# Moving half of the first MLP weight to the head of the load stream of a decode kernel

## The chip, the core and the metric

The kernel runs on one core of a Trainium2 chip. The metric is device time in microseconds (us). The kernel before takes 77.36 us, the median of 13 runs that lie between 77.12 and 78.14 us. The execution that the profiler recorded took 77.22 us; the recorded span, from the first instruction to the last, is 75.5 us.

The engines are called as the profile calls them: PE is the matrix engine (PEld its weight loads), DVE the vector engine, ACT the scalar engine, POOL the general one, and SP the engine that here does nothing but issue DMAs. Sixteen DMA engines of the core move what the DMA instructions ask for; "SPq" is SP's queue of issuing instructions.

## The reference

One decode step for a batch of four tokens with 512 features. The input is layer-normed; the result goes through two branches, and the output is `x + s * g`:

- attention `s`: `q = xn @ wq` gives 32 query heads of 128; 8 key/value heads serve four query heads each. Only the last 1024 of 4096 cached positions are used. Scores `q·k / sqrt(128)`, softmax, product with V, and `@ wo`, a 4096 x 512 matrix.
- MLP gate `g`: the input is normed once more, `h = gelu(y @ w1 + b1)` with `w1` 512 x 1792, `silu(h @ w2 + b2)` with `w2` 1792 x 512.

All arrays are bf16. What has to be read from DRAM is about 28.8 MB: 8 K blocks and 8 V blocks of 1 MB each, `wq` and `wo` of 4 MB each, `w1` and `w2` of 1.75 MB each, and some vectors.

## The kernel before

The program is a list of operations for each engine, in the order in which the Python code adds them; `add` puts one on a compute engine, `dma` one on the queue of an issuing engine, each with the operations it depends on. There is no scheduler: an engine runs its list from top to bottom, and `emit` puts a wait ahead of an operation for every dependency on another engine or a DMA.

All large loads are issued by SP, so their order is the order of the load stream. Before the change it is K0, K1 (L216, L217), the two halves of `wq` (L219), K2 to K7 (L221), V0 (L440), `w1` whole (L441), V1 (L443), `w2` (L444), V2 to V7 (L446), and `wo` in six pieces (L453), the last of them small. K and V share eight buffers of 1 MB: V of head g is loaded into the buffer that held K of head g, so its issue waits for the last transposes of that K block (L214). Nothing else in the stream before the output waits for a compute engine. ACT issues the small loads.

A K block has 128 partitions, each holding 32 consecutive positions of one batch entry, a contiguous 8 KB row in DRAM. The four partitions next to each other are the four batch entries, 8 MB apart in DRAM. `w1` is laid out with four rows of the matrix to a partition: 14 KB contiguous in DRAM, one partition behind the other.

PE's list is:

1. eight transpose units T(0) to T(7) (K0 and K1, four units of eight 128x128 transposes each, L279), copied to SBUF by DVE (L285);
2. the transposes of the normed input (L347);
3. the query product in two halves, each waiting for its half of `wq` (L362), copies of the result by DVE and ACT (L368, L369), and its transposes (L374);
4. 32 pairs of T(n) and S(n-8): a unit of transposes, and the score matmuls of a unit that was transposed eight units earlier (L294 sets the mask, L298 multiplies); the exponential of a head's scores is taken by ACT (L306);
5. for each head g, PV(g) (L316) and the sum of the probabilities (L322), with DVE's epilogue one head behind (L329 to L334). Behind PV(0) stands the first MLP product (L392, L394), which waits for `w1`; behind PV(1) the second one (L419, L421), which waits for `w2`;
6. a rearrangement of the attention result (L465, copied at L472), and the product with `wo`, one group of matmuls for each of its six pieces (L486), each waiting for its piece;
7. the gate, a transpose, the residual and the output DMA (L512 to L520).

The two lines of the wait that ties the V loads to PE, and those of the `w1` load and its only reader:

```python
            kv_buf[:, (HKV + g) % NS, :, :].rearrange("p c d -> p (c d)"), cache_rows(A_v_cache, g)),
            t_last[(HKV + g) % NS] if HKV + g >= NS else None)
...
    d_w1 = pg.dma("sp", "w1", lambda e: e.dma_start(
        w1_sb[:, :, :], B_w1.rearrange("(p c) f -> p c f", c=4)))
...
        t = add("pe", fn, v_xyT, d_w1, d_b1)
```

Of the kernel before, what the change touches and what calls it, by code (L numbers as in the profile page):

```python
# [16 lines left out]
class _Program:  # L17
# [10 lines left out]
    def add(self, eng, fn, *deps):  # L28
        op = _Op(eng, fn, deps)
        self.ops[eng].append(op)  # L30
        return op
# [42 lines left out]
def bass_recurrent_scan__sliding_block_cached__mixer_channel_mlp__decode_kernel(  # L74
# [48 lines left out]
    w1_sb = sb([128, 4, F], BF16)  # L123
# [63 lines left out]
    pg = _Program(nc)  # L187
    add = pg.add
# [3 lines left out]
    d_b1 = pg.dma("act", "b1", lambda e: e.dma_start(  # L192
        b1_sb[0:1, :], B_b1.rearrange("(o n) -> o n", o=1)))
# [3 lines left out]
    def cache_rows(cache, g):  # L197

        return bass.AP(cache.tensor, g * SK * DH + WS * DH,
                       [[NC * DH, KR], [HKV * SK * DH, B], [1, NC * DH]])  # L200
# [5 lines left out]
    def load_k(g):  # L206
        d_k[g] = pg.dma("sp", "k%d" % g, lambda e: e.dma_start(  # L207
            kv_buf[:, g, :, :].rearrange("p c d -> p (c d)"), cache_rows(A_k_cache, g)),
            )

    def load_v(g):
        d_v[g] = pg.dma("sp", "v%d" % g, lambda e: e.dma_start(  # L212
            kv_buf[:, (HKV + g) % NS, :, :].rearrange("p c d -> p (c d)"), cache_rows(A_v_cache, g)),
            t_last[(HKV + g) % NS] if HKV + g >= NS else None)  # L214

    load_k(0)  # L216
    load_k(1)  # L217
    wq_r = A_wq.rearrange("(p c) n -> p c n", c=4)
# [120 lines left out]
    v_xyT = None  # L339
# [14 lines left out]
    v_xyT = add("dve", lambda e: e.tensor_copy(yT[:, :], psK[1][:, 16:32]), t_xy)  # L354
# [31 lines left out]
    def mlp1():  # L386
        def fn(pe):
            last = None
            for k in range(FC):
                o = psM[:, PS_H + k * 4:PS_H + (k + 1) * 4]  # L390
                for c in range(4):
                    pe.matmul(o, bass.AP(w1_sb, c * F + k, [[4 * F, 128], [FC, 128]]),  # L392
                              yT[:, c * 4:(c + 1) * 4], start=(c == 0), stop=False)
                last = pe.matmul(o, bass.AP(b1_sb, k, [[F, 1], [FC, 128]]), ones_bf[0:1, 0:4],  # L394
                                 start=False, stop=True)
            return last
        h = psM[:, PS_H:PS_H + FC * 4]
        t = add("pe", fn, v_xyT, d_w1, d_b1)
        a = add("act", lambda e: e.activation(u2_sb[:, :], h, AF.Square), t)  # L399
        v = add("dve", lambda e: e.tensor_scalar(t_sb[:, :], u2_sb[:, :], GELU_K, 1.0,  # L400
                                                 op0=ALU.mult, op1=ALU.add), a)
        v = add("dve", lambda e: e.tensor_tensor(t2_sb[:, :], t_sb[:, :], h, ALU.mult), v)
        mlp["e"] = add("act", lambda e: e.activation(ge_sb[:, :], t2_sb[:, :], AF.Exp,
                                                     scale=-GELU_A), v)
# [31 lines left out]
    for n in range(LAG, NUN + LAG):  # L436
# [1 line left out]
            T(n)  # L438
        S(n - LAG)
    load_v(0)  # L440
    d_w1 = pg.dma("sp", "w1", lambda e: e.dma_start(  # L441
        w1_sb[:, :, :], B_w1.rearrange("(p c) f -> p c f", c=4)))
    load_v(1)  # L443
    d_w2 = pg.dma("sp", "w2", lambda e: e.dma_start(  # L444
        w2_sb[:, :, :], B_w2.rearrange("(p c) o -> p c o", c=FC)))
# [49 lines left out]
    for g in range(HKV):  # L495
        PV(g)
        if g == 0:
            mlp1()
        if g >= 1:
            epilogue(g - 1)  # L500
        if g == 1:
            mlp2()
            mlp3()
        if g == 2:
            mlp4()
    epilogue(HKV - 1)
    rows = to_rows(0, HKV)
    for k in range(len(d_wo)):
# [7 lines left out]
    t = add("pe", lambda pe: pe.transpose(psS[0][0:16, 0:128], sg_sb[:, :], ident32[:, :]),  # L516
            v, c_id32, ex[HKV - 2])
# [56 lines left out]
```

## Time and profile before

| | us |
|---|---|
| median of 13 runs | 77.36 |
| lowest and highest run | 77.12, 78.14 |
| the profiled execution | 77.22 |
| its span | 75.5 |
| PE busy | 55.2 |
| DVE busy | 38.1 |
| ACT busy | 9.0 |

The DMA engines' packets of SP's queue fill 91.7% of the span of sixteen engines, and 28.85 MB are read from DRAM, 382 GB/s over the span. The page divides the span into 40 slices; each digit is the busy share of an engine in a slice, in tenths. The row PEclk is the clock that PE was granted, in tenths of full speed. A waiting instruction is shown with the idle time ahead of it and, behind an arrow, with what ended it; "issue" stands for time in which the profile shows nothing that the engine waits for.

### The profile page before, as it was taken

The page shows a single profiled execution, that of the slowest core. Times are in us where ns is not written, and L with a number is a line of the kernel's source. Part 1 is how long each engine was busy: PE and PEld are TensorE (multiplying, and loading weights), DVE is VectorE, ACT ScalarE, POOL GpSimd, SP SyncE. Part 2 cuts the span into 40 slices and gives each one's busy share as a digit, 9 for nine tenths or more (in the row PEclk, how much of TensorE's full clock was granted, in tenths as well). Part 3 has the DMA queues.
Part 4 walks back from the last instruction along what each step waited for, and adds up shares of the span by engine and source line. Part 5 has one row for each costly group of instructions (what it writes and reads, how often), then busy time and mean ns, then how long its engine had stood idle before and what let it go on. Part 6 is the DMA issues. An engine that isn't in the chain of part 4 may idle for free.

```text
span 75.5 us, 2408 instructions
## 1 busy us (share of the span) xinstructions
PE 55.2 (73%) x1107; PEld 47.0 (62%) x1107; DVE 38.1 (50%) x84; ACT 9.0 (12%) x16; POOL 4.5 (6%) x13
## 2 busy tenths in 40 slices
PE   0009994603689999999999909999299999728850
PEld 0009993201078999999998809999098675428730
DVE  0678988100323999999985000003943968850010
ACT  0611000000360213203204400002000000000000
POOL 6970000000000000000000000000000000000000
PEclk9999999996555999999999985555555555555555
DMA  0899999999999999999999999999999999999600
GB/s 2 275 404 417 445 452 425 425 425 395 430 425 430 425 417 438 417 430 449 428 394 451 422 433 396 425 417 425 430 425 434 408 408 425 410 415 422 249 15 2
DMA packets 4213, 28.99 MB, mean 384 GB/s; under 512 B 486, under 2 KB 619, under 8 KB 1644
## 3 DMA queue, kind: packets, MB, share of 16 engines
q1 hardware_dynamic: 4160, 28.84, 91.7%
q8 instruction: 8, 0.13, 0.6%
q10 hardware_dynamic: 44, 0.01, 0.1%
q14 instruction: 1, 0.01, 0.0%
HBM read 28.85 MB, written 0.00 MB: 382 GB/s over the span
## 4 chain that ended last, share of the span: by engine, by line
DMA 49%; PE 25%; SPq 21%; issue 1%; DVE 1%
DMA kv_buf<-in_A_k_cache_dram 25%; DMA wo_sb<-in_A_wo_dram 24%; SPq L454 17%; PE psK L279 16%; PE psS L298 6%; PE psS L294 2%; SPq L207 2%; SPq L219 1%; PE psM L486 1%; PE psS L516 1%; SPq L212 0%; DVE o_bf L518 0%; DVE sg_sb L512 0%
## 5 line engine op out<-in xcount | busy, mean ns | idle before, releaser
L279 PE MATMUL psK<-ident,kv_buf 128*128 128x128 bf16 x256 | 21.6, 241 | 5.9 <-DMA kv_buf<-in_A_k_cache_dram 5.8
L285 DVE COPY kt_buf<-psK 128x1024 bf16<-128x1024 bf16 x32 | 21.0, 688 | 2.8 <-PE psK L279 2.7
L279 PEld LDWEIGHTS psK<-ident,kv_buf 128*128 128x128 bf16 x256 | 17.5, 109 | 6.3 <-DMA kv_buf<-in_A_k_cache_dram 6.1
L298 PE MATMUL psS<-qT,kt_buf 128*128 128x16 bf16 x256 | 10.3, 170 | 0.0
L298 PEld LDWEIGHTS psS<-qT,kt_buf 128*128 128x128 bf16 x256 | 9.5, 97 | 1.1 <-issue 0.3
L316 PEld LDWEIGHTS psO<-P_buf,kv_buf 128*128 128x128 bf16 x256 | 7.7, 103 | 2.2 <-issue 1.9
L316 PE MATMUL psO<-P_buf,kv_buf 128*128 128x16 bf16 x256 | 8.2, 174 | 0.3
L392 PE MATMUL psM<-yT,w_sb 128*128 128x4 bf16 x56 | 5.7, 204 | 1.8 <-issue 1.8
L306 ACT ACTIVATE P_buf<-psS 128x512 bf16<-128x512 f32 x8 | 4.8, 597 | 16.1 <-PE psS L298 16.1
L329 DVE TENSOR_REDUCE den_sb<-psS 128x16 f32<-128x512 f32 x8 | 5.5, 688 | 1.7 <-PE psS L322 1.4
L392 PEld LDWEIGHTS psM<-yT,w_sb 128*128 128x128 bf16 x56 | 4.5, 153 | 2.3 <-issue 2.1
L400 DVE TENSOR_SCALAR t_sb<-u_sb 128x56 f32<-128x56 f32 x1 | 0.2, 192 | 11.4 <-ACT u_sb L399 11.4
L362 PE MATMUL psO<-wq_sb,xT 128*32 128x512 bf16 x32 | 2.9, 505 | 3.8 <-DMA wq_sb<-in_A_wq_dram 3.5
L486 PE MATMUL psM<-OW,wo_sb 128*128 128x4 bf16 x128 | 4.0, 166 | 1.5 <-DMA wo_sb<-in_A_wo_dram 1.0
L486 PEld LDWEIGHTS psM<-OW,wo_sb 128*128 128x128 bf16 x128 | 3.7, 104 | 1.8 <-DMA wo_sb<-in_A_wo_dram 1.2
L322 PE MATMUL psS<-P_buf,ones_bf 128*128 128x512 bf16 x8 | 4.5, 561 | 0.0
L362 PEld LDWEIGHTS psO<-wq_sb,xT 128*32 128x32 bf16 x32 | 0.8, 112 | 5.1 <-DMA wq_sb<-in_A_wq_dram 4.0
L368 DVE CAST q_sb<-psO 128x512 bf16<-128x512 f32 x1 | 0.7, 690 | 6.5 <-PE psO L362 6.5
L294 PE MATMUL psS<-negm,ind 128*128 128x512 bf16 x8 | 3.3, 410 | 0.0
L419 PE MATMUL psM<-hT,w_sb 128*128 128x4 bf16 x56 | 2.1, 167 | 1.4 <-DVE hT L411 1.4
L394 PE MATMUL psM<-ones_bf,b_sb 1*128 1x4 bf16 x14 | 3.0, 215 | 0.0
L419 PEld LDWEIGHTS psM<-hT,w_sb 128*128 128x128 bf16 x56 | 1.8, 105 | 1.9 <-DVE hT L411 1.9
(63 smaller groups left out, 28.7 us busy)
## 6 DMA issues: line engine op xcount, KB each, us to landing
kv_buf<-in_A_k_cache_dram SPq DMA_DIRECT2D x8, 1024.0 KB, 21.4
kv_buf<-in_A_v_cache_dram SPq DMA_DIRECT2D x8, 1024.0 KB, 23.7
wq_sb<-in_A_wq_dram SPq DMA_DIRECT2D x2, 2048.0 KB, 13.3
w_sb<-in_B_w_dram SPq DMA_DIRECT2D x2, 1792.0 KB, 31.0
wo_sb<-in_A_wo_dram SPq DMA_DIRECT2D x3, 1024.0 KB, 24.9
wo_sb<-in_A_wo_dram SPq DMA_DIRECT2D x1, 512.0 KB, 21.5
wo_sb<-in_A_wo_dram SPq DMA_DIRECT2D x1, 384.0 KB, 18.2
wo_sb<-in_A_wo_dram SPq DMA_DIRECT2D x1, 128.0 KB, 18.0
```

The lines of the kernel that those rows point to most:

```text
L279: last = pe.transpose(psK[n % NB][:, j * 128:(j + 1) * 128], kv_buf[:, g, u * UT + j, :], ident[:, :])
L285: cp[n] = add("dve", lambda e: e.tensor_copy(kt_buf[:, n % NKT, :], psK[n % NB][:, 0:1024]), t, sc.get(n - NKT))
L294: pe.matmul(psS[g % 2][:, 0:512], ind[:, :], negm[:, :], start=True, stop=False, skip_group_check=True)
L298: last = pe.matmul(psS[g % 2][:, c * 16:(c + 1) * 16], kt_buf[:, n % NKT, j * 128:(j + 1) * 128], qT[:, g * 16:(g + 1) * 16], start=False, ...
L306: ex[g] = add("act", lambda e: e.activation(P_buf[:, g, :], psS[g % 2][:, 0:512], AF.Exp, scale=SCALE), sc[n])
L316: last = pe.matmul(pso[:, 0:16], kv_buf[:, (HKV + g) % NS, c, :], P_buf[:, g, c * 16:(c + 1) * 16], start=(c == 0), stop=(c == NC - 1))
L322: den[g] = add("pe", lambda pe: pe.matmul(psS[g % 2][:, 0:512], ones_bf[:, :], P_buf[:, g, :], start=True, stop=True), ex[HKV - 2 + g % 2] ...
L329: v = add("dve", lambda e: e.tensor_reduce(den_sb[:, cs], bass.AP(psS[g % 2], 0, [[512, 128], [1, 16], [16, NC]]), AX.X, ALU.add), den[g])
L392: pe.matmul(o, bass.AP(w1_sb, c * F + k, [[4 * F, 128], [FC, 128]]), yT[:, c * 4:(c + 1) * 4], start=(c == 0), stop=False)
L419: pe.matmul(o, w2_sb[:, k, c * 128:(c + 1) * 128], hT[:, k * 4:(k + 1) * 4], start=(k == 0), stop=False)
L454: e.dma_start(wo_sb[:, g0:g1, i0:i1, :], wo_r[:, g0:g1, i0:i1, :]))))
L486: last = pe.matmul(psM[:, PS_W + c * 4:PS_W + (c + 1) * 4], wo_sb[:, g, i, c * 128:(c + 1) * 128], OW[:, i, g * 4:(g + 1) * 4], start=firs ...
```

## The change

The load of `w1` is cut in two DMAs of two matrix rows to a partition (7 KB in DRAM and in SBUF for each of the 128 partitions). The first is issued by SP ahead of everything else, before K0. The second stays at the place of the old load, between V0 and V1. The first MLP product now waits for both. No compute instruction changes or moves in its engine's list.

```diff
+    w1_r = B_w1.rearrange("(p c) f -> p c f", c=4)
+
+    def load_w1(c):
+        return pg.dma("sp", "w1%d" % c, lambda e: e.dma_start(
+            w1_sb[:, 2 * c:2 * c + 2, :], w1_r[:, 2 * c:2 * c + 2, :]))
+
+    d_w1 = [load_w1(0)]
     load_k(0)
     load_k(1)
...
-        t = add("pe", fn, v_xyT, d_w1, d_b1)
+        t = add("pe", fn, v_xyT, *d_w1, d_b1)
...
     load_v(0)
-    d_w1 = pg.dma("sp", "w1", lambda e: e.dma_start(
-        w1_sb[:, :, :], B_w1.rearrange("(p c) f -> p c f", c=4)))
+    d_w1.append(load_w1(1))
     load_v(1)
```

## The prediction

> **What bounds the kernel now.** I read the page's busy slices and DMA part first, then the stretches, the chain of waits, the list of PE's waits, and the timeline at the places they point to.
>
> ```profile
> span 75.5 us, 2408 instructions
> ...
> PE   0009994603689999999999909999299999728850
> ...
> DMA  0899999999999999999999999999999999999600
> ...
> q1 hardware_dynamic: 4160, 28.84, 91.7%
> ```
>
> The DMA row is full from the second slice to the 36th: the load stream hardly pauses, and its end is close to the kernel's end. Bytes do not change, so a gain can come only from the rate. The stretches (us, busy times by engine, granted clock, DMA share, GB/s) show where the rate is low:
>
> ```profile
> 2.00:8.00 6.00, 2.25 (x22) 2.25 (x23) 4.79 (x13) 1.69 (x3) 3.12 (x6) 1.00 1.03 394
> 8.00:17.00 9.00, 5.30 (x69) 4.31 (x67) 4.89 (x10) 0.00 (x0) 0.00 (x0) 1.00 1.00 426
> 26.00:40.00 14.00, 13.95 (x323) 13.24 (x321) 12.97 (x20) 2.98 (x5) 0.00 (x0) 1.00 1.01 424
> 53.00:70.00 17.00, 13.08 (x340) 10.23 (x340) 10.20 (x31) 0.18 (x1) 0.00 (x0) 0.50 1.01 419
> ```
>
> Only the opening is slow: 394 against 426 GB/s over 6 us is 6 x (1 - 394/426) = 0.45 us of stream. K and V blocks run at 424 later on, `wo` (4 KB rows and shorter, with some V) at 419.
>
> The chain that ended last, in order of time (start, us, what), and PE's own list of waits:
>
> ```profile
> 3.30 18.67 DMA kv_buf<-in_A_k_cache_dram
> ...
> 22.02 1.03 PE psK L279 x8
> 23.06 0.43 PE psS L294
> 23.48 0.20 PE psS L298 x8
> ...
> 24.70 0.46 PE psK L279 x8
> ...
> 53.90 18.20 DMA wo_sb<-in_A_wo_dram
> ```
>
> ```profile
> PE psK L279 <- DMA kv_buf<-in_A_k_cache_dram: 5.8, 1, 5.8
> PE psO L362 <- DMA wq_sb<-in_A_wq_dram: 3.5, 1, 3.5
> ...
> PE psM L486 <- DMA wo_sb<-in_A_wo_dram: 1.0, 3, 0.4
> ```
>
> PE waits for data three times: for K0 at the start, for the second half of `wq` (until 18.19 us), and for `wo` at the end. Between 18.19 and the first `wo` group it waits for no V block, no `w1`, no `w2`: one long chain of matmuls and DVE copies. So there are two chains, the stream and the matmuls, and the last wait tells how far apart they end. The timeline of the end:
>
> ```profile
> 67.71 1.84 PE L486 MATMUL psM<-OW,wo_sb 128*128 128x4 bf16 x64 [0.51 <-DVE OW L472]
> 69.97 1.01 PE L486 MATMUL psM<-OW,wo_sb 128*128 128x4 bf16 x32 [0.42 <-DMA wo_sb<-in_A_wo_dram]
> 71.20 0.59 PE L486 MATMUL psM<-OW,wo_sb 128*128 128x4 bf16 x16 [0.21 <-DMA wo_sb<-in_A_wo_dram]
> 72.15 0.59 PE L486 MATMUL psM<-OW,wo_sb 128*128 128x4 bf16 x16 [0.36 <-DMA wo_sb<-in_A_wo_dram]
> ```
>
> The stream wins, but only by 0.42 + 0.21 + 0.36 = 0.99 us. If the matmul chain comes later by more than 0.99 us, it sets the end.
>
> **The change, part by part.**
>
> *The 7 KB rows ahead of K0.* Half of `w1` is 917,504 bytes; at 426 GB/s that is 2.15 us. K0, K1, both halves of `wq` and K2 to K7 land 2.15 us later; from V1 on the stream stands where it stood. This delays what the matmul chain starts on: the second half of `wq` released PE at 18.19 us, and K2 landed at 3.30 + 18.67 = 21.97, just before T(8) at 22.02. Both move, so neither absorbs the shift. +2.15 us on the matmul chain.
>
> *What `w1` buys.* Nothing waits for it before. Its load was issued at 9.96 us and took 31.0 us to land, at 40.9; the first product's first matmul ran at 43.13. The 1.83 us gap of PE at 45.12, put down to "issue", lies behind that first matmul, which had already read `w1`, so it is no wait for the load. Gain 0.
>
> *One more DMA on SP.* An issue of this size takes 0.6 us (two K issues in 1.25 us), ahead of K0 and of each later issue. The 2.15 us of transfer of the new first load cover it; without that cover K0 would be 0.6 us later. V0's issue waits for T(3) and moves from 9.38 to about 11.5 us; it took 27 us from issue to landing, so what hides it is a backlog of more than 20 us. The same holds at the end: V7's issue at 40.06 waits for PE's last transposes and goes to about 42.2, and the `wo` issues behind it move too; they landed 18.0 us or more after issue, which leaves 16 us. ACT's and POOL's queues have nothing moved.
>
> *Shorter rows.* The two halves are 256 rows of 7 KB in place of 128 of 14 KB. Between the rows at 426 GB/s and those at 419, 1.8 MB cost 0 to 0.07 us; I take 0.03.
>
> *The opening.* The loss of 0.45 us may belong to K0's and K1's rows, as the first loads: then `w1` in front cures it, -0.45. It may belong to whatever opens the stream: 0. Or `w1`'s opening loses as much and K's does too: +0.45. The nearest row, K blocks of the same layout at 424 GB/s in 26 to 40 us, says that the layout loses nothing by itself, so I take 0.
>
> [...]
>
> *The matmul clock.* The stretches at one microsecond give the granted clock's switches (the clock is the third number from the end of a line):
>
> ```profile
> 17.00:18.00 1.00, 0.00 (x0) 0.00 (x0) 0.00 (x0) 0.00 (x0) 0.00 (x0) 0.76 0.88 369
> 24.00:25.00 1.00, 1.00 (x23) 1.00 (x20) 0.45 (x1) 0.00 (x0) 0.00 (x0) 0.83 1.03 434
> 44.00:45.00 1.00, 0.00 (x0) 0.00 (x0) 0.00 (x0) 0.00 (x0) 0.00 (x0) 0.91 0.97 416
> ```
>
> With two levels, 1.0 and 0.5, the clock fell at 17.52, rose at 24.34 and fell at 44.82; the distances 6.82 and 20.48 are 1 to 3, so the switches may lie on a grid of 6.8 us or a fraction of it. From 18.19 to 24.34 the chain runs 6.15 us at half clock. There a pair of T and S costs 1.03 + 0.20 = 1.23 us against 0.46 + 0.18 = 0.64 later: each microsecond at half clock loses 0.48. If the switches move along with the work: 0. If they stay on a grid of half of 6.82, the slow stretch may last from 3.4 to 6.8 us: -1.3 to +0.3, on average -0.5. I take half of that, -0.25.
>
> [...]
>
> *Sum.* Matmul chain: +2.15 + 0.03 - 0.25 = +1.93; less the 0.99 us that it was early: +0.94 us at the end. The stream itself: 0 to 0.05. The profiled execution's 77.22 becomes 78.16; it lies 0.14 below the median of 77.36, against which I put the forecast at 78.2.
>
> **The rivals.** A difference within 0.5% (0.39 us) is about what a measurement of this kernel cannot tell from no change.
>
> *Faster: the clock comes back one step sooner.* Place: 18 to 26 us. Price: 3.41 x 0.48 = -1.6 us on the matmul chain, more than the +1.19 by which it would otherwise be late (2.15 + 0.03 - 0.99). Then the stream sets the end again, and a cured opening shows: 77.36 - 0.45 = 76.9. It decides from 1.19/0.48 = 2.5 us less at half clock. For it: 6.15 us is near the top of what the grid allows. Against it: it needs the opening cured as well, for which only 0.45 us are there.
>
> *Hidden anyway.* The same, with the opening as slow as before, or a late chain of less than 0.4 us: 77.0 to 77.7, say 77.4.
>
> *Not what it says.* `w1` in front opens as badly and the clock stays low one step more: 2.18 - 0.99 + 1.6 = +2.8, 80.1. [...]
>
> **How the numbers follow.** Matmul chain late and deciding: 0.60, with 77.75 to 78.8 (the upper end: 77.36 + 1.19 + 0.3 for the clock). Hidden anyway: 0.22. Faster: 0.15. Slow twice: 0.03. The range that holds 8 in 10 goes from 76.95, the case of a cured opening, to 78.85; the likeliest case's own is 77.75 to 78.8. Faster by over 0.5%: 0.15; within: 0.23; slower: 0.62.
>
> **What the profile after would show.** PE's wait for the second half of `wq` ends near 20.3 us instead of 18.19, the wait for K0 near 7.9 instead of 5.75. The first `wo` group starts between 69 and 70.2 us instead of 67.71, and PE no longer waits 1.0 us for `wo`, or hardly. The last piece of `wo` still lands between 71.8 and 72.6 us. The stretch from 2 to 8 us tells of the opening: 394 GB/s again if it belongs to any first load, some 415 or more if K0 at the head was the cause. The prediction is wrong if the `wo` waits are still there: then either the chain started less late than 2.15 us, or the half-clock stretch was shorter by 2.5 us.

## The result, and the profile after

The changed kernel is slower: the ratio to the kernel before is 1.0114, with a 95% interval of 1.0067 to 1.0162, so 77.36 us become about 78.2 us. A second measurement on another occasion gave 1.0102 (1.0035 to 1.0169). The ratios leave out the runs classed as slow, and these are most runs of the changed kernel: over all 11 timed ones its median is 79.15 us (77.73 to 80.36), against 77.36 us (77.05 to 78.93) in 48 runs of the kernel before. So the loss is 0.9 us by the ratio and 1.8 us by all runs, and the changed kernel spreads over 2.6 us, where the kernel before spreads over 1.9.

The profiled execution of the changed kernel is its best: 77.28 us, a span of 75.6 us, hardly more than the 77.22 and 75.5 us of the kernel before. Its time does not show the loss, but its lines show what decides now. From the page:

```profile
span 75.6 us, 2409 instructions
...
PE   0000799470278999999999982999929999946970
...
DMA  1899999999999999999999999999999999999500
...
q1 hardware_dynamic: 4304, 28.84, 91.8%
...
PE 60%; DMA 23%; DVE 7%; issue 4%; SPq 3%; ACT 0%
DMA wq_sb<-in_A_wq_dram 23%; PE psK L286 16%; PE psO L323 8%; PE psS L305 8%; PE psM L399 6%; PE psM L492 5%; PE psS L329 4%; PE psM L401 3%; PE psS L301 3%; PE psM L426 3%; PE psO L369 3%; DVE den_sb L336 2%; SPq L207 2%; PE psK L381 1%; DVE q_sb L375 1%
```

The stream is as full as before (91.8% against 91.7%). But the chain that ended last runs over PE for 60% of the span, and its only transfer is `wq`; before, the last piece of that chain was `wo` and 24% of the span. PE's waits (what waited, for whom, us in total, times, longest) and the timeline of the query product and of `wo`:

```profile
PE psK L286 <- DMA kv_buf<-in_A_k_cache_dram: 8.1, 1, 8.1
PE psO L369 <- DMA wq_sb<-in_A_wq_dram: 3.4, 1, 3.4
```

```profile
20.29 1.90 PE L369 MATMUL psO<-wq_sb,xT 128*32 128x512 bf16 x16 [3.38 <-DMA wq_sb<-in_A_wq_dram]
...
69.06 3.69 PE L492 MATMUL psM<-OW,wo_sb 128*128 128x4 bf16 x128 [0.51 <-DVE OW L478]
```

The wait for `wo` is gone. All 128 matmuls of `wo` run in one piece of 3.69 us, and their data has landed before they are due. K0 releases PE 2.31 us later than before (8.06 against 5.75), the second half of `wq` 2.10 us later (20.29 against 18.19), T(8) 1.80 us later (23.82 against 22.02), and the first `wo` group starts 1.35 us later (69.06 against 67.71). The stretches:

```profile
2.00:8.00 6.00, 0.00 (x0) 0.00 (x0) 4.55 (x12) 1.63 (x3) 3.12 (x6) 1.00 0.94 377
8.00:17.00 9.00, 7.50 (x88) 6.53 (x88) 5.58 (x10) 0.00 (x0) 0.00 (x0) 1.00 1.03 440
26.00:40.00 14.00, 14.00 (x324) 13.41 (x322) 12.89 (x20) 2.98 (x5) 0.00 (x0) 0.98 1.01 423
53.00:70.00 17.00, 13.60 (x343) 10.44 (x343) 11.02 (x33) 0.65 (x3) 0.00 (x0) 0.50 1.01 418
```

The rates are those of before, within what a stretch's borders do. (The 377 GB/s from 2 to 8 us are neither of the two values that the prediction named; the stream starts before 2 us now, and its borders no longer fit this stretch.) From 0 to 17 us the mean is 371 GB/s against 365, which is 0.1 MB or 0.24 us ahead; the last piece of `wo` landed 14.7 us after its issue at 57.53, at 72.2, against 54.38 + 18.0 = 72.4 before. The stream gained 0.2 us that nobody waits for.

### The profile page after: what moved, and what is told of

It reads as the page before. It is cut to its first block, busy times and chain, and to the rows that moved or that the text cites. A ratio compares the mean times of both kernels' runs of the same rounds, so it can differ in the third digit from the quotient of the medians.

```text
span 75.6 us, 2409 instructions
## 1 busy us (share of the span) xinstructions
PE 54.4 (72%) x1107; PEld 46.7 (62%) x1107; DVE 38.5 (51%) x84; ACT 9.0 (12%) x16; POOL 4.5 (6%) x13
## 3 DMA queue, kind: packets, MB, share of 16 engines
q1 hardware_dynamic: 4304, 28.84, 91.8%
## 4 chain that ended last, share of the span: by engine, by line
PE 60%; DMA 23%; DVE 7%; issue 4%; SPq 3%; ACT 0%
DMA wq_sb<-in_A_wq_dram 23%; PE psK L286 16%; PE psO L323 8%; PE psS L305 8%; PE psM L399 6%; PE psM L492 5%; PE psS L329 4%; PE psM L401 3%; PE psS L301 3%; PE psM L426 3%; PE psO L369 3%; DVE den_sb L336 2%; SPq L207 2%; PE psK L381 1%; DVE q_sb L375 1%
## 6 DMA issues: line engine op xcount, KB each, us to landing
wo_sb<-in_A_wo_dram SPq DMA_DIRECT2D x3, 1024.0 KB, 24.1
```

## The experiments

Two theories besides the late matmul chain (theory 1) had to be told apart: that the extra DMA and its shorter rows slow the stream (theory 2), and that any load but K0 at the head opens it badly (theory 3).

**The two halves, but both at the old place.**

```diff
-    d_w1 = [load_w1(0)]
+    d_w1 = []
...
+    d_w1.append(load_w1(0))
     d_w1.append(load_w1(1))
```

> The first MLP weight is cut in the same two DMAs of 7 KB rows, but both stand where the whole load stood, between V0 and V1. Theory 1 (the data that the matmul chain starts on come 2.15 us later, and the chain sets the end): nothing is ahead of K0, so no difference from before, 77.2 to 77.5 us, PE waits about 1.0 us for wo. Theory 2 (the extra DMA and its shorter rows slow the stream): as slow as the changed kernel, 78 to 79 us, with the last piece of wo landing later than 72.4 us. Theory 3 (the stream opens differently): no difference here.

77.38 us, ratio 1.0013 (0.9993 to 1.0032): the cut by itself costs nothing that shows, and theory 2 falls. But the profile isn't what was expected. PE did not wait for `wo` there; the second half of `wq` released it at 19.72 us instead of 18.19, though nothing in the stream ahead of it differs from before. The two `wq` loads' time from issue to landing, before and here:

```profile
DMA to landing us min/median/max: 11.1/13.3/15.4
```

```profile
DMA to landing us min/median/max: 11.1/14.0/16.9
```

The first half landed equally fast, the second 1.5 us later. A load lands in 16 shares, each with its own time in the trace; 15 of this one had landed by 18.09 us, the last one at 19.68. A 16 KB packet of the instruction queue (the page counts it to the same sixteen DMA engines) starts in this execution at 17.6 to 17.7 us, before the second half is in; in the kernel before it starts at 18.0 to 18.1, when the second half is nearly in, and there K2's last share is the late one (21.98 against 20.59 us for the fifteenth). That the packet makes the share late fits in time: in all thirteen profiles no load ahead of the first such packet has a last share more than 0.5 us behind the fifteenth, and the load that is landing at the packet, or the next one, has one 0.8 to 1.6 us behind. But the packet itself took only 0.96 us here, and moving it wasn't tried, so the cause is not shown.

The half-clock stretch is longer as well. The clock is the third number from the end:

```profile
17.00:18.00 1.00, 0.00 (x0) 0.00 (x0) 0.00 (x0) 0.00 (x0) 0.00 (x0) 0.94 0.97 401
28.00:29.00 1.00, 0.95 (x24) 0.88 (x22) 0.99 (x2) 0.60 (x1) 0.00 (x0) 0.94 1.04 442
```

By the two-level reading it fell at 17.9 and rose at 28.1: 10.2 us, against 6.8 before. So this execution's chain was late by 1.5 us and some slow microseconds more, and ended the kernel instead of the stream: a span of 75.9 us against 75.5, with the load order of before.

**How much of the weight goes first.** A quarter (the cut after one matrix row of four), and the whole weight as one DMA:

```diff
-    def load_w1(c):
+    def load_w1(c, cut=1):
+        lo, hi = ((0, cut), (cut, 4))[c]
...
-            w1_sb[:, 2 * c:2 * c + 2, :], w1_r[:, 2 * c:2 * c + 2, :]))
+            w1_sb[:, lo:hi, :], w1_r[:, lo:hi, :]))
```

```diff
-            w1_sb[:, 2 * c:2 * c + 2, :], w1_r[:, 2 * c:2 * c + 2, :]))
+            w1_sb[:, :, :], w1_r[:, :, :]))
...
-    d_w1.append(load_w1(1))
```

> Only one of the four matrix rows of a partition (3.5 KB rows, a quarter of the weight) opens the stream, the other three follow between V0 and V1. Theory 1: the second half of wq lands 1.08 us later than before instead of 2.15; the chain was 1.0 to 1.3 us early, so the end is 77.2 to 77.8 us, with PE's waits for wo down to 0.3 us or less. Theory 3 (any foreign first load costs, by how the stream opens): the same loss as with half of the weight, 78 to 79 us.

> The whole weight opens the stream (14 KB rows, one DMA, the number of DMAs as before). Theory 1: the second half of wq lands 4.3 us later than before, near 22.5 us; chain late by 4.3 - 1.3 = 3.0 us, so 80.0 to 81.5 us, with no wait for wo left. Theory 2 (an extra DMA, shorter rows): no more DMAs and no shorter rows than before, so 77.4 us. Theory 3: as the changed kernel, 78 to 79 us.

The quarter: 78.06 us, ratio 1.0101 (1.0051 to 1.0151). The whole: 82.03 us, ratio 1.0608 (1.0549 to 1.0666). The whole has no more DMAs than before and its old rows, which settles theory 2, and it costs far more than half does, against theory 3, by which the loss should not depend on the amount. The quarter's time alone would fit theory 3, as it loses what the half loses; its profile and the two next experiments speak for theory 1. But the quarter lost more than theory 1 gave it, and so did the whole (4.7 us against an expected 2.6 to 4.1). The profiles show the same two additions as above. PE's query product and `wo` in the two kernels, quarter first:

```profile
20.66 1.90 PE L370 MATMUL psO<-wq_sb,xT 128*32 128x512 bf16 x16 [5.20 <-DMA wq_sb<-in_A_wq_dram]
...
69.53 3.69 PE L493 MATMUL psM<-OW,wo_sb 128*128 128x4 bf16 x128 [0.51 <-DVE OW L479]
```

```profile
24.68 1.90 PE L369 MATMUL psO<-wq_sb,xT 128*32 128x512 bf16 x16 [5.30 <-DMA wq_sb<-in_A_wq_dram]
...
74.17 3.55 PE L491 MATMUL psM<-OW,wo_sb 128*128 128x4 bf16 x128 [0.51 <-DVE OW L477]
```

20.66 is 18.19 + 1.08 + 1.4, and 24.68 is 18.19 + 4.3 + 2.2. The half-clock stretch behind it ends at 27.9 and at 31.7 us, 7.2 and 7.0 us after `wq`'s release instead of 6.15. In both the last share of the second half of `wq` landed well behind the other fifteen (20.62 against 19.15 us, and 24.64 against 23.05), with an instruction packet that starts at 18.1 and at 22.6 us.

**A late chain with the stream of before.** Ten matmuls that nobody reads, reckoned as 2.1 us at half clock (2.3 us in the profile), ahead of the rearrangement:

```diff
+    def f_late(pe):
+        last = None
+        for _ in range(10):
+            last = pe.matmul(psM[:, 256:512], ones_bf[:, :], negm[:, 0:256], start=True, stop=True)
+        return last
+    add("pe", f_late, ep[HKV - 1])
     rows = to_rows(0, HKV)
```

> The kernel before, its load stream untouched, with ten matmuls of 256 columns (read by nobody) on PE behind the last head's epilogue, ahead of the rearrangement and wo: at half clock 10 x 0.21 = 2.1 us on the matmul chain, as much as the change puts on its start. Theory 1 (a late matmul chain is enough): slower by 2.1 less the 1.0 to 1.3 us that the chain was early, 78.2 to 79.2 us, no wait for wo left. Rival (the loss is in the stream, not in PE): 77.4 us.

78.73 us, ratio 1.0166 (1.0095 to 1.0237): as expected. In the profile `wo` starts 2.7 us later than before (70.42), more than the ten matmuls took, because the second half of `wq` was 1.3 us late here too (19.50). PE waits for no piece of `wo`, and the last piece landed at 72.2, no later than before. A late chain is enough for a loss of this size, with the load stream left as it was.

**The late data with a shorter chain.** In both kernels half of the first MLP product's matmuls are left out, so the output lacks half of that sum:

```diff
-                for c in range(4):
+                for c in range(2):
                     pe.matmul(o, bass.AP(w1_sb, c * F + k, [[4 * F, 128], [FC, 128]]),
```

> The kernel before with the first MLP product over two of the four matrix rows of a partition (28 of its 56 matmuls left out, so the output lacks half of that sum; the load stays whole). It takes some 2.5 us off the matmul chain and nothing off the stream. Theory 1: the stream sets the end as before, 77.2 us, with the slowest runs gone; PE waits for wo for 2 to 3 us.

> The changed kernel with the same 28 matmuls left out (the output lacks half of that sum; both loads stay). Theory 1: the chain is 2.15 us late and 2.5 us shorter, the stream sets the end again, so 76.9 to 77.4 us: within 0.4 us of the kernel before with the same cut, and some 1.5 us under the changed kernel. Rival (the stream itself has become slower): 78 us or more, with wo's last piece landing late. What is left between this and the other cut kernel is what the new opening is worth to the stream alone.

With the order of before 77.14 us (77.05 to 77.26), ratio 0.9960 (0.9933 to 0.9987); with the changed order 77.41 us (77.09 to 78.85), ratio 0.9998 (0.9956 to 1.0041). So the changed load order costs 0.3 us by the medians once the chain is shorter, instead of 0.9 to 1.8 us, and most of the loss isn't in the stream. PE waits for `wo` again, in the changed order with the cut by less than in the order of before:

```profile
PE psM L492 <- DMA wo_sb<-in_A_wo_dram: 0.6, 2, 0.4
```

```profile
PE psM L486 <- DMA wo_sb<-in_A_wo_dram: 1.1, 3, 0.5
```

The 2 to 3 us of waiting that I expected of the cut kernel of before are 1.1, in part because this execution's clock rose only at 25.9, 1.55 us later than in the kernel before, or some 0.7 us of work. Two more things follow. The kernel before, too, is held up by its matmul chain in some runs: with the chain cut it loses 0.4% and its upper tail. And the gain of 0.2 us in the opening doesn't show here: in the two profiles the last piece of `wo` landed at 72.4 us with the order of before and at 72.7 with the changed one.

**Matmuls in the gap.** The changed kernel, with 24 matmuls of 256 columns on constants between the halves of the query product:

```diff
+    def f_warm(pe):
+        last = None
+        for _ in range(24):
+            last = pe.matmul(psM[:, 256:512], ones_bf[:, :], negm[:, 0:256], start=True, stop=True)
+        return last
+    add("pe", f_warm, c_neg)
     t_q = add("pe", lambda pe: f_q(pe, 1), d_wq[1])
```

> The changed kernel with 24 matmuls of 256 columns on constants (their result is read by nobody) between the two halves of the query product, where PE waits for the second half of wq; they take 2.6 us at full clock, inside the gap of 3.4 us. Theory 1 with the clock: the half-clock stretch of some 6 us behind the gap goes, the chain gains up to 6.2 x 0.48 = 2.9 us, more than it is late; PE waits for wo again and the time is 77.0 to 77.4 us, with little spread. If the clock isn't what spreads the runs: 78 to 79 us as without them. If the matmuls themselves delay the chain: above 79 us.

78.52 us, ratio 1.0182 (1.0116 to 1.0248): a miss. The gap was filled and the second half of the product took 1.05 us instead of 1.90, but the timeline goes on like this:

```profile
20.35 1.05 PE L369 MATMUL psO<-wq_sb,xT 128*32 128x512 bf16 x16 [0.36 <-DMA wq_sb<-in_A_wq_dram]
22.20 0.62 PE L388 MATMUL psK<-ident,q_sb 128*128 128x128 bf16 x8 [0.80 <-DVE q_sb L382]
23.77 0.76 PE L286 MATMUL psK<-ident,kv_buf 128*128 128x128 bf16 x8 [0.96 <-DMA kv_buf<-in_A_k_cache_dram]
24.75 0.40 PE L305 MATMUL psS<-qT,kt_buf 128*128 128x16 bf16 x8 [0.22 <-issue]
25.01 1.01 PE L286 MATMUL psK<-ident,kv_buf 128*128 128x128 bf16 x8
```

What was gained was lost at once in a wait for K2, T(8) starting at 23.77 as in the changed kernel (23.82), and the clock fell afterwards, at 24.1, for 3.4 us. Behind that this execution lost more: `wo` starts at 69.96 against 69.06, and PE's gaps put down to "issue" are 2.4 us at PV, where the changed kernel has 1.7 us at the first MLP product. So the run neither frees the chain of the clock nor tells what a freed chain would do.

**Work in the gap instead.** What PE needs late should come late, and what it waits for early. K0 and K1 are not used until the query exists; so the first half of `wq` opens the stream, then come K0, K1, and the second half, and PE transposes K0 and K1 in the gap. The essence (T(1) and the query's transposes get the waits that their shared buffer then needs):

```diff
+    d_wq = [load_wq(0)]
     load_k(0)
     load_k(1)
+    d_wq.append(load_wq(1))
...
-    for n in range(LAG):
-        T(n)
...
     add("pe", lambda pe: f_q(pe, 0), v_xT, d_wq[0])
+    for n in range(LAG):
+        T(n)
     t_q = add("pe", lambda pe: f_q(pe, 1), d_wq[1])
```

> The kernel before with the first half of wq as the first load, then K0, K1, the second half of wq and the rest as it was; on PE the small transposes and the first half of the query product stand ahead of T(0), which is behind them. Nothing that the chain needs lands later than before at 18.2 us, K0 and K1 land 4.9 us later, and PE transposes them in the gap in which it waited for wq, so that gap is filled. Theory 1 with the clock: the half-clock stretch behind 18.2 us shrinks or goes, the chain is earlier by 1 to 3 us, the stream decides: 77.0 to 77.3 us, few slow runs. If any load of another kind than K at the head costs (theory 3): 78 us or more.

> The kernel in which the first half of wq opens the stream, once more, for its interval: 0.3 to 0.7% faster than before, 77.0 to 77.3 us, PE waits for wo by 1 us or more, full clock at 18 us.

77.15 us, ratio 0.9948 (0.9914 to 0.9982), and again 77.25 us, ratio 0.9978 (0.9953 to 1.0003): 0.2 to 0.5% under the kernel before (the second interval just reaches no change), with nothing above 77.8 us. The first profile, in which the clock stayed at 1.0 from 14.6 to 45.3 us, shows what it buys:

```profile
8.53 1.90 PE L364 MATMUL psO<-wq_sb,xT 128*32 128x512 bf16 x16 [0.45 <-DMA wq_sb<-in_A_wq_dram]
18.10 1.05 PE L364 MATMUL psO<-wq_sb,xT 128*32 128x512 bf16 x16 [1.74 <-DMA wq_sb<-in_A_wq_dram]
67.04 1.84 PE L490 MATMUL psM<-OW,wo_sb 128*128 128x4 bf16 x64 [0.51 <-DVE OW L476]
```

The chain is 0.67 us earlier at `wo` (67.04 against 67.71) and PE waits 1.4 us for it. So the stream bounds the kernel here, and an earlier chain can gain no more. In the second profile the clock did fall, for 6.8 us, and the wait was 1.0 us. A foreign load at the head that does not make the chain late costs nothing, which is against theory 3 once more.

**The 2.15 us once more, in that order.** Half of `w1` ahead of it, the other half at the old place (shown against the kernel just above):

```diff
+    d_w1 = [load_w1(0)]
     d_wq = [load_wq(0)]
     load_k(0)
```

> Half of the first MLP weight opens the stream as in the changed kernel, then the first half of wq, K0, K1, the second half of wq and the rest; PE's order as in the run in which wq opens. The data of the chain come 2.15 us later as in the changed kernel, but the gap ahead of the query product is filled with the transposes of K0 and K1, so it should run at full clock. Theory 1 with the clock: the chain, 1.4 to 1.8 us early in that run, becomes 0.3 to 0.8 us late: 77.3 to 78.0 us, under the changed kernel by 1 us or so. If only the 2.15 us count and not the clock: as the changed kernel, 78.3 to 79.2 us.

> The changed kernel once more, beside the next two on the same chip. Theory 1: 78 to 79.5 us, PE waits for no piece of wo, the second half of wq releases PE at 20.3 us or, where an instruction fetch of 16 KB sits in the queue of one DMA engine ahead of it, up to 1.5 us later; the half-clock stretch behind it lasts 6.8 or 10.2 us. The time follows these two: with 6.8 us and 20.3 near 77.3, with both bad near 80.

Side by side on one chip: 77.93 us with the filled gap, ratio 1.0024 (0.9974 to 1.0075), against 78.86 us of the changed kernel, ratio 1.0102 (1.0035 to 1.0169). The `wq` half came as late in both (20.76 and 20.35 us), and what differs is that K0 and K1 come behind the first half of `wq` and fill PE's gap, and the clock with it: in the profile of this kernel it is 1.0 from 16.9 to 47.6 us. Each run's mean granted clock is on record: the five of its ten runs with 0.808 or more took 77.21 to 77.78 us, the five with 0.780 or less 78.07 to 78.91. By the medians, filling the gap takes away 0.9 of the 1.5 us that `w1` at the head costs on this chip; the two intervals overlap. The profile of the changed kernel in this measurement has the early release (20.35) and a slow stretch of 6.8 us, and took 77.50 us, as expected for that case.

## Why the prediction was right

- **The bound and the shift.** Right. Forecast +2.15 us at the second half of `wq`, measured +2.10; forecast about 7.9 us for K0, measured 8.06. The matmul chain became the bound and the wait for `wo` went.
- **"Both move, so neither absorbs the shift."** Not so. Before, T(8) had itself waited for K2's late share:

```profile
22.02 0.77 PEld L279 LDWEIGHTS psK<-ident,kv_buf 128*128 128x128 bf16 x8 [0.36 <-DMA kv_buf<-in_A_k_cache_dram]
```

K2's last share moved by 1.80 us only (21.98 to 23.78), and T(8) with it. Between T(8) and `wo` another 0.45 us of the delay went, in three short gaps that the changed kernel's execution did not have, or had shorter (0.2 us at 38.7, 0.1 at the first MLP product, 0.25 at 60.5). So in the profiled pair the chain was 1.35 us late at `wo`, where the sum has 1.93.
- **What `w1` buys.** Nothing, as said. PE's 1.8 us "issue" gap in the first MLP product is still there (1.7 us), so it wasn't the load.
- **SP's queue and the row size.** Costs of nothing and of 0.03 us: the run with both halves at the old place agrees, 1.0013.
- **The opening.** Taken as 0; 0.2 us better in the profiled pair, not visible in the times of the cut kernels, and nothing like the 0.45 us of the cured opening that the faster rival needed.
- **The 0.99 us by which the chain was early.** Too small. Added up from PE's waits, it took the four groups of `wo` as fixed; without the waits all 128 matmuls take 3.69 us and would have ended at 67.71 + 3.69 = 71.40 instead of 72.74: 1.34 us early. The four groups took 4.03 us as pieces; the 0.35 us that being in pieces cost had been counted as work.
- **The clock's -0.25.** Wrong in sign, and its upper bound too low. I let the slow stretch behind the release of `wq` last 3.4 to 6.8 us. The profiles with the old gap have 6.1 to 8.4 us (19.50 to 25.6 with the late end, 20.29 to 26.56 in the changed kernel, 19.72 to 28.1 with both halves at the old place), against 6.15 in the kernel before: the 3.4 us with the gaps around the query product in them (PE busy for 1.9 us of them in the kernel before, 2.1 in the changed one) were not followed by full clock. One slow step more, as the last rival has it, did come, though in neither profile of the changed kernel itself: in six of the other profiles the clock stayed low for 10.2 us, through a second 3.4 us in which PE was busy for 1.9 to 2.6 us.
- **The term that was missing.** One share of the second half of `wq` landed 1.4 to 1.6 us behind the other fifteen in four of the profiled variants (both halves at the old place, the late end, quarter, whole), and 0.8 us in the changed kernel with the shorter product, presumably behind an instruction packet. Before, 1.3 us of slack can take it up; afterwards nothing does. In both profiles of the changed kernel itself it was K2 that had the late share.
- **The sum.** 78.2 us, measured 77.36 x 1.0114 = 78.24 by the ratio; the median of all its runs, 79.15, lies above the 78.85 up to which the prediction goes. The mechanism carries the direction, but the close agreement is in good part luck, errors against each other: in the profiled pair the chain was 1.35 us late against a slack of 1.34, so the loss of 0.94 us that the sum gives was not there (77.28 against 77.22), and what the other runs lose must come on top. The slow clock and the late share can each put 1 us or more on the chain (8.4 us at half clock instead of 6.15, with 0.48 lost in each; a share 1.4 to 1.6 us late). Which of them did in the timed executions wasn't recorded; the mean granted clock speaks for the first, as it is 0.766 to 0.773 in the three runs up to 78.1 us and 0.747 to 0.759 in the nine above. In the second measurement one run does not fit: 80.42 us at 0.763.

## What to carry to other kernels

When a load stream and a compute chain end within a microsecond or so of each other, the order of the stream must be read from the chain's side: a load that nobody waits for may not stand ahead of one that somebody does, even with the stream always full and its length unchanged. Look in the profile for what the first long wait is for, load that first, and put work that needs other data into the wait. To find the slack between two chains, reckon when the last groups would end if nothing held them; the sum of their waits was too small here (0.99 us against 1.34). And a profile of one execution can miss a loss that most runs have (here 77.28 us against a median of 79.15): compare its time with theirs.

## What the runs showed of the hardware

- The granted clock switched on a grid: the stretches between switches were 3.4, 6.8, 10.2, 20.5 and 30.7 us, multiples of 3.41, and the grid stood differently to the program in each execution (first rise between 8.6 and 16.9 us). The page and the views show 1.0 ahead of the first rise, but there PE ran slowly too: in the kernel before, the first transposes follow each other at 106 ns, behind the rise at 56.
- Stretches of 3.4 us at half clock with part of the query product in them and 0.8 us of waiting for its copies were not followed by full clock (PE busy for 1.9 of 3.4 us in the kernel before, 2.6 of 3.4 in the second profile of the changed one). Up to 45 us, in all thirteen profiles, no stretch of 3.41 us at half clock with PE busy for 2.66 us or less, by the profile, was followed by full clock, and each with 2.74 us or more was. Behind 45 us, in the matmuls of 4 and 16 columns, stretches that were busy throughout were not followed by it either (in the kernel before, PE was busy from 48.24 to 51.65 us without a pause and the clock stayed at 0.50 to the end). With K0 and K1 ahead of the query product, none of the profiles got the clock back before 6.1 us had passed from `wq`'s release, except where matmuls had kept it up.
- The first DMA's data moved from 1.8 us with `w1` at the head and from 2.2 us with K0, both issued at 0.80: its issue on SP took 0.39 against 0.61 us. The first half of `wq` at the head behaved like `w1` (0.39 us, data from 1.8). Why wasn't tried.
- Instruction packets of 16 KB, eight in an execution (nine in the one with matmuls in the gap), ran beside a full load stream, and in these executions one share of a 1 or 2 MB load landed 0.8 to 1.6 us behind the other fifteen where the first such packet ran as it landed or shortly before; that the packet is the cause is argued from the times, not shown.
